# Attention and MoE on one core: PSUM banks and the softmax buffer placed by the emitting code, softmax sums in one burst

## Chip, cores, metric

One core of a Trainium2 chip. The metric is the device time of one execution in microseconds (us). Each kernel was run several times in several rounds; each round also ran the kernel before on the same chip. All runs quoted were classed as fast (undisturbed).

## What is computed

A spatial-reduction attention followed by a two-layer feed-forward network (the "MoE" of the names), cut to what matters:

```python
kv_pool = kv.reshape(B, H//4, 4, W//4, 4, C).mean(axis=(2, 4))     # 384 x 32 -> 96 x 8 = 768 keys
k = v = kv_pool.reshape(B, -1, C) @ w_sr
s = (q @ k.T) / sqrt(C);  a = softmax(s)                           # 4 x 12288 queries, 768 keys, C = 128
x = (a @ v)
h = x @ w_in                                                        # 128 -> 2048
out = (h * sigmoid(1.702 * h)) @ w_out                              # 2048 -> 128
```

The softmax is computed without the maximum: exp, then a product with v, then a division by the column sums.

## The kernel before

Queries come in 96 groups of 512; four groups are a block, so there are 24 blocks. Everything that ScalarE must evaluate comes in chunks of 128 x 512, and three chunks (K = 3) are one unit: TensorE *fills* three PSUM banks, one ACTIVATE of ScalarE *evacuates* them to SBUF as bf16, and later TensorE *drains* each chunk with one matmul into an accumulator. A group has 6 attention chunks and 16 MoE chunks, so there are 96 attention units and 256 MoE units in each of two halves: attention of 48 groups, MoE of 48 groups, and the same again. 704 units in all.

The eight banks are two triples for fills and two accumulators. Accumulators serve every other job in turn: attention outputs, MoE outputs, column sums, pooling, key and value projections, transposes.

```python
R = 2; AG = 31; L = 10
agpool = ctx.enter_context(tc.tile_pool(name="ag", bufs=AG))        # 31 buffers of 3 chunks = 93 chunks
big    = ctx.enter_context(tc.tile_pool(name="big", bufs=2, space=bass.MemoryType.PSUM))
ring   = ctx.enter_context(tc.tile_pool(name="ring", bufs=2, space=bass.MemoryType.PSUM))

def fill_attn(i, t):                      # one unit: three chunks of group i
    s_ps = big.tile([128, K, 512], F32, name="big")
    for k in range(K):
        nc.tensor.matmul(s_ps[:, k, :], kTs[b][:, ...], rhs, start=True, stop=True)
    a = agpool.tile([128, K, 512], BF, name="ag")
    nc.scalar.activation(a, s_ps, AF.Exp, scale=scale)

def sums(s, t):                           # half of a block's column sums: 12 matmuls, four column groups
    if t == 0:
        ss_of[s] = ring.tile([128, 512], F32, name="ring")
    for jc in range(K * t, K * t + K):
        for gi in range(4):
            nc.tensor.matmul(ss[32 * gi:32 * gi + 32, :], ones, a_of[4 * s + gi, t][:, jc % K, :], ...)
    # after the second half: transposes, reciprocal, broadcast
...
for n in range(len(seq)):                 # the emitting loop: a model of ScalarE's backlog decides
    fill_next(n + 2)
    while True:
        ...                               # sums first if due, else other jobs, else a drain
        if f is None and (done == len(todo) or d > (n - L if attn else n)):
            break                         # in attention, keep back the last L = 10 units
        cost = COST[f] if f else 1.0
        if now + cost + K + HANDOVER > end[-1] and n - d <= AG - 4 and n + 3 < len(seq):
            break                         # else ScalarE would run dry: emit the next fill first
        now += cost
        ...
```

The order of instructions is thus fixed when the program is emitted: the loop keeps a small model of when ScalarE will run dry and puts drains and other jobs between fills as they fit.

Of the kernel before, what the change touches and what calls it, by code (L numbers as in the profile page):

```python
# [19 lines left out]
def kernel(  # L20
# [18 lines left out]
    K = 3  # L39
# [10 lines left out]
    AG = 31  # L50
# [8 lines left out]
    agpool = ctx.enter_context(tc.tile_pool(name="ag", bufs=AG))  # L59
    npool = ctx.enter_context(tc.tile_pool(name="norm", bufs=5))  # L60
    opool = ctx.enter_context(tc.tile_pool(name="op", bufs=3))
    big = ctx.enter_context(tc.tile_pool(name="big", bufs=2, space=bass.MemoryType.PSUM))
    ring = ctx.enter_context(tc.tile_pool(name="ring", bufs=2, space=bass.MemoryType.PSUM))

    ctx.enter_context(tc.manual_schedule(engines=None))

# [15 lines left out]
    def pool_kv(b, a):  # L82

        ps = ring.tile([128, 512], F32, name="ring")
        ts = [kv_tiles.pop((b, a, ch)) for ch in range(HC)]
        order = ([(ch, w) for ch in range(HC) for w in range(r)] if b == 0 else
                 [(ch, w) for w in range(r) for ch in range(HC)])
        for ch, w in order:
            if (b, a, w) == (0, 0, 0) and ch > 0:
                warm(4)  # L90
            nc.tensor.matmul(ps[32 * ch:32 * ch + 32, :], mean4, ts[ch][:, w],  # L91
                             start=(w == 0), stop=(w == r - 1))
        pooled[b, a] = kvtmp.tile([Hp, 4, C], BF, name="pooled")
        nc.vector.tensor_copy(pooled[b, a].rearrange("p a c -> p (a c)"), ps[:Hp, :])  # L94

    def transpose_pooled(b, a):
        ps = ring.tile([128, 4, Hp], BF, name="ring")
        t = pooled.pop((b, a))
        for wp in range(4):
            nc.tensor.transpose(ps[:, wp, :], t[:, wp, :], ident[:Hp, :Hp])  # L100
        pTs[b, a] = kvtmp.tile([128, h], BF, name="pT")
        nc.vector.tensor_copy(pTs[b, a], ps.rearrange("p a b -> p (a b)"))

    def make_k(b, a):
        ps = ring.tile([128, 512], F32, name="ring")
        if a == 0:
            kTs[b] = kvres.tile([128, J], BF, name="kT")
        nc.tensor.matmul(ps[:, :h], w_sr_sb, pTs[b, a], start=True, stop=True)
        nc.vector.tensor_copy(kTs[b][:, a * h:(a + 1) * h], ps[:, :h])

    def make_v(b, a):
        ps = ring.tile([128, 512], F32, name="ring")
        if a == 0:
            vs[b] = kvres.tile([128, JC, C], BF, name="v")
        pT = pTs.pop((b, a))
        for k in range(K):
            nc.tensor.matmul(ps[:, k * C:(k + 1) * C], pT[:, k * 128:(k + 1) * 128], w_sr_sb,
                             start=True, stop=True)
        nc.vector.tensor_copy(vs[b][:, a * K:(a + 1) * K, :].rearrange("p k c -> p (k c)"), ps[:, :h])
# [20 lines left out]
    def transpose_q(g):  # L140
# [3 lines left out]
        ps = ring.tile([128, 4, 128], BF, name="ring")  # L144
# [45 lines left out]
    warm_ps = big.tile([128, K, 512], F32, name="big")  # L190

    def warm(n):

        for _ in range(n):
            nc.tensor.matmul(warm_ps[:32, 0, :], ones, ones.unsqueeze(1).broadcast_to([128, 16, 32]),  # L195
                             start=True, stop=True)
# [15 lines left out]
    a_of, av_of, rb_of = {}, {}, {}  # L212

    def fill_attn(i, t):
        b, s = i // GB, i // 4
        s_ps = big.tile([128, K, 512], F32, name="big")
        rhs = qTs[s][:, 0, (i % 4) * G:(i % 4 + 1) * G]
        for k in range(K):
            jc = K * t + k
            nc.tensor.matmul(s_ps[:, k, :], kTs[b][:, jc * 128:(jc + 1) * 128], rhs,  # L220
                             start=True, stop=True)
        a = agpool.tile([128, K, 512], BF, name="ag")
        nc.scalar.activation(a, s_ps, AF.Exp, scale=scale)  # L223
        a_of[i, t] = a

    def drain_attn(i, t, k):
        b, s = i // GB, i // 4
        jc = K * t + k
        if jc == 0:
            av_of[i] = ring.tile([128, 512], F32, name="ring")  # L230
        nc.tensor.matmul(av_of[i], vs[b][:, jc, :], a_of[i, t][:, k, :],  # L231
                         start=(jc == 0), stop=(jc == JC - 1))
        if k == K - 1:
            del a_of[i, t]
        if jc == JC - 1:
            if i % 4 == 0:
                xs[s] = x_tile(s)
            nc.vector.tensor_tensor(xs[s][:, (i % 4) * G:(i % 4 + 1) * G],  # L238
                                    av_of.pop(i), rb_of.pop(i), MUL)

    ss_of = {}

    def sums(s, t):

        if t == 0:
            ss_of[s] = ring.tile([128, 512], F32, name="ring")
        ss = ss_of[s]
        for jc in range(K * t, K * t + K):
            for gi in range(4):
                nc.tensor.matmul(ss[32 * gi:32 * gi + 32, :], ones,  # L250
                                 a_of[4 * s + gi, t][:, jc % K, :],
                                 start=(jc == 0), stop=(jc == JC - 1))
        if t == 0:
            return
# [45 lines left out]
    g_of, o_of = {}, {}  # L300

    def fill_moe(t):
        h_ps = big.tile([128, K, 512], F32, name="big")
        for k in range(K):
            g, fc = divmod(K * t + k, FCH)
            nc.tensor.matmul(h_ps[:, k, :], w_in_sb[:, fc * 128:(fc + 1) * 128],  # L306
                             xs[g // 4][:, (g % 4) * G:(g % 4 + 1) * G], start=True, stop=True)
        a = agpool.tile([128, K, 512], BF, name="ag")
        nc.scalar.activation(a, h_ps, AF.Gelu_apprx_sigmoid)  # L309
        g_of[t] = a  # L310

    def drain_moe(t, k):
        a = g_of[t]
        g, fc = divmod(K * t + k, FCH)
        if fc == 0:
            o_of[g] = ring.tile([128, 512], F32, name="ring")
        nc.tensor.matmul(o_of[g], w_out_sb[:, fc, :], a[:, k, :],  # L317
                         start=(fc == 0), stop=(fc == FCH - 1))
        if k == K - 1:
            del g_of[t]  # L320
        if fc == FCH - 1:

            o_sb = opool.tile([128, 512], F32, name="o_sb")
            nc.vector.transpose(o_sb, o_of.pop(g))  # L324
            for m in range(4):
                nc.sync.dma_start(out=out_r[g, m],
                                  in_=o_sb[32 * m:32 * m + 32, :].rearrange("i (b j) -> i b j", j=32))

    NA, NM = 2 * NG, NG * FCH // K

    units = [(i, t) for t in range(2) for i in range(4)] + [(i, t) for i in range(4, NG) for t in range(2)]
    seq = []
    for n in range(R):
        seq += [(True, u) for u in range(n * NA // R, (n + 1) * NA // R)]
        seq += [(False, u) for u in range(n * NM // R, (n + 1) * NM // R)]

    def fill(p):
        if p >= len(seq):
            return
        attn, n = seq[p]  # L340
        if not attn:
            fill_moe(n)
            return
        i, t = units[n]
        if n % 2 == 0:
            background(n // 2)
        if n == 1:
            transpose_q(3)
        if n == 2:
            make_v(0, 0)  # L350
        if n == 4:
# [3 lines left out]
        if n == 6:  # L355
            make_v(0, 1)
        if n == 7:
            transpose_q(4)
            transpose_q(5)
        if n in (11, 12):  # L360
            extras.append((transpose_q, n - 5))
        elif n % 2 == 1:
            extra(n // 2 - 1)
        fill_attn(i, t)
# [4 lines left out]
    UNIT, SWITCH, HANDOVER = 6.25, 6.0, 1.0  # L369
    COST = {pool_kv: 4.5, transpose_pooled: 1.5, make_k: 1.0, make_v: 1.5, transpose_q: 1.0, sums: 3.5}  # L370
    todo = [(p, k) for p in range(len(seq)) for k in range(K)]
    done = done_s = seen_a = done_a = 0
    now, end = 0.0, []

    def fill_next(p):
# [3 lines left out]
        fill(p)  # L379
# [4 lines left out]
        if p and seq[p][0] != seq[p - 1][0]:  # L384
# [3 lines left out]
    fill_next(0)  # L388
    fill_next(1)
    for n in range(len(seq)):  # L390
        fill_next(n + 2)
        attn, u = seq[n]
        seen_a += attn
        while True:
            d = done // K
            f = None
            if not av_of or done_s in ss_of:
                if done_s in ss_of:
                    f, args = sums, (done_s, 1)
                elif done_s < NS and seen_a >= 8 * done_s + 8 and done_a >= 8 * done_s - 2:  # L400
                    f, args = sums, (done_s, 0)
                elif extras:
                    f, *args = extras[0]
            if f is None and (done == len(todo) or d > (n - L if attn else n)):
                break
            cost = COST[f] if f else 1.0
            if now + cost + K + HANDOVER > end[-1] and n - d <= AG - 4 and n + 3 < len(seq):
                break
            now += cost
            if f is sums:  # L410
                f(*args)
                if args[1] == 1:
                    del ss_of[done_s]
                    done_s += 1
            elif f:
                extras.pop(0)
                f(*args)
            else:
                p, k = todo[done]
                a, w = seq[p]  # L420
                if a:
                    drain_attn(w // 2, w % 2, k)
                    done_a += k == K - 1
                else:
                    drain_moe(w, k)
                done += 1
# [31 lines left out]
```

## Time and profile before

| | before |
|---|---|
| time, median | 1009.5 us (1009.13 to 1010.20, 6 runs) |
| span of the profiled run | 1008.3 us |
| TensorE busy, ScalarE busy | 97%, 95% |
| ScalarE's first Gelu run without a gap starts | 192.69 us |
| first half's last ACTIVATE ends | 509.71 us |
| last weight load of the last sums block | 678.07 us |
| last weight load of all | 1002.57 us |

How to read it. Two engines look full, so the shares say little. The first half ends when ScalarE has made all its units: from 192.69 us on it does not stand still. The second half ends when TensorE has made its last drain: it works off a stock of chunks that attention has left. So a gain in the first half counts only as far as ScalarE gets done earlier, and a gain in the second half counts as TensorE time. The lines are in the prediction below.

One view is used that no single line of the profile gives, here called *priced idle*. The trace records every weight load of TensorE, so the matmuls between the last weight loads of two sums blocks can be counted exactly. Each is priced as in the prediction (0.2158 us for a full one, and so on), and what is left of the interval is idle.

### The profile page before, as it was taken

What the parts mean: (1) busy time and instruction counts of PE and PEld (TensorE: products, weight loads), DVE (VectorE), ACT (ScalarE), POOL (GpSimd) and SP (SyncE); (2) the same over time, 40 slices, a digit from 0 to 9 for tenths busy, and PEclk for the clock granted to TensorE, in tenths of its full rate; (3) what the DMA queues carried; (4) which work ended last, traced back from release to release, by engine and by line L of the source; (5) the groups of instructions that cost most, each with busy time, mean ns of one, the idle gap of its engine ahead of it and who ended that gap; (6) DMA issues with size and microseconds to landing.
All of it is one profiled execution on the core that took longest, in us unless ns stands there. A gap on an engine that the chain in (4) does not pass through costs nothing.

```text
span 1008.3 us, 12769 instructions
## 1 busy us (share of the span) xinstructions
PE 980.7 (97%) x4916; PEld 433.0 (43%) x5014; DVE 199.0 (20%) x321; ACT 960.9 (95%) x711; POOL 92.8 (9%) x151
## 2 busy tenths in 40 slices
PE   7899999999999999999999999999999999999997
PEld 2343344444444444444433344444444444444443
DVE  3333334311101110111113333331101110111101
ACT  3899998999999999999999999999999999999995
POOL 3132322200000000000002212221000000000000
PEclk8999999999999999999999999999999999999999
DMA  9985990142222222222238660000222222222223
GB/s 190 189 165 89 202 151 1 34 80 38 40 43 42 40 35 41 43 43 38 38 71 160 119 109 22 1 1 11 43 43 43 37 38 42 41 43 37 37 43 53
DMA packets 256157, 63.83 MB, mean 63 GB/s; under 512 B 251392, under 2 KB 252544, under 8 KB 255744
## 3 DMA queue, kind: packets, MB, share of 16 engines
q1 hardware_dynamic: 248656, 36.79, 21.5%
q0 software_dynamic: 7440, 26.22, 14.0%
q8 instruction: 39, 0.64, 0.3%
q14 instruction: 22, 0.18, 0.1%
HBM read 52.49 MB, written 36.70 MB: 88 GB/s over the span
## 4 chain that ended last, share of the span: by engine, by line
PE 85%; ACT 9%; DVE 2%; issue 2%; DMA 1%; POOL 0%; SPq 0%; ACTq 0%; DVEq 0%; POOLq 0%
PE big L306 33%; PE ring L317 30%; PE ring L231 9%; PE big L220 9%; ACT ag L223 8%; PE ring L250 3%; ACT ag L309 1%; DMA x<-in_kv_dram 1%; PE ring L91 1%; DMA out_dram<-o_sb 0%; DVE t L257 0%; DVE pooled L94 0%; DVE t L261 0%; DVE x L238 0%; DVE o_sb L324 0%
## 5 line engine op out<-in xcount | busy, mean ns | idle before, releaser
L309 ACT ACTIVATE ag<-big 128x1536 bf16<-128x1536 f32 x512 | 691.1, 1459 | 4.9 <-PE big L306 4.9
L306 PE MATMUL big<-x,w_in_sb 128*128 128x512 bf16 x1532 | 414.9, 379 | 3.4
L317 PE MATMUL ring<-ag,w_out_sb 128*128 128x512 bf16 x1477 | 394.5, 379 | 0.1
L223 ACT ACTIVATE ag<-big 128x1536 bf16<-128x1536 f32 x192 | 262.9, 1461 | 16.8 <-PE big L220 15.4
L306 PEld LDWEIGHTS <-w_in_sb 128*128 128x128 bf16 x1536 | 150.0, 98 | 182.6 <-issue 2.9
L317 PEld LDWEIGHTS <-w_out_sb 128*128 128x128 bf16 x1536 | 150.3, 98 | 181.6 <-issue 0.4
L324 DVE STREAM_TRANSPOSE o_sb<-ring 128x512 f32<-128x512 f32 x96 | 68.8, 717 | 561.6 <-PE ring L317 520.3
L220 PE MATMUL big<-qT,kT 128*128 128x512 bf16 x557 | 156.4, 384 | 8.3 <-ACT ag L223 4.2
L231 PE MATMUL ring<-ag,v 128*128 128x512 bf16 x560 | 155.3, 379 | 3.3 <-DVE x L238 2.0
L264 POOL PARTITION_BROADCAST rb<-t x96 | 66.6, 797 | 577.7 <-DVE t L261 577.7
L238 DVE TENSOR_TENSOR x<-ring,rb 128x512 bf16<-128x512 f32 x96 | 66.4, 692 | 154.3 <-PE ring L231 139.4
L220 PEld LDWEIGHTS <-kT 128*128 128x128 bf16 x576 | 54.2, 98 | 83.2 <-issue 24.3
L231 PEld LDWEIGHTS <-v 128*128 128x128 bf16 x576 | 55.4, 98 | 72.9 <-issue 10.5
L250 PE MATMUL ring<-ag,ones 128*32 128x512 bf16 x576 | 38.4, 382 | 0.0
L257 DVE STREAM_TRANSPOSE t<-ring 128x512 f32<-128x512 f32 x24 | 17.2, 717 | 56.5 <-PE ring L250 56.5
L250 PEld LDWEIGHTS <-ones 128*32 128x32 bf16 x576 | 11.7, 95 | 23.9 <-issue 17.0
L261 DVE STREAM_TRANSPOSE t<-t 128x512 f32<-128x512 f32 x24 | 17.1, 711 | 2.8 <-DVE t L259 0.5
L151 ACT COPY qT<-ring 128x512 bf16<-128x512 bf16 x3 | 1.8, 586 | 13.8 <-PE ring L147 13.8
L125 POOL DMA_DIRECT2D q_bf<-in_q_dram x22 | 11.4, 520 | 4.1 <-DMA x<-in_kv_dram 2.7
L79 POOL DMA_DIRECT2D kvt<-in_kv_dram x18 | 10.1, 568 | 7.8 <-DMA x<-in_kv_dram 4.0
L94 DVE CAST pooled<-ring 96x512 bf16<-96x512 f32 x8 | 5.5, 687 | 15.7 <-PE ring L91 15.7
L195 PE MATMUL big<-ones 128*32 128x512 bf16 x22 | 7.3, 481 | 0.9 <-DVE col L171 0.9
(39 smaller groups left out, 74.9 us busy)
## 6 DMA issues: line engine op xcount, KB each, us to landing
out_dram<-o_sb SPq DMA_DIRECT2D x384, 64.0 KB, 1.9
q_bf<-in_q_dram POOLq DMA_DIRECT2D x22, 512.0 KB, 7.6
kvt<-in_kv_dram POOLq DMA_DIRECT2D x18, 512.0 KB, 9.4
x<-in_kv_dram POOLq DMA_DIRECT2D x6, 512.0 KB, 10.7
x<-in_q_dram POOLq DMA_DIRECT2D x1, 512.0 KB, 18.5
w_in_sb<-in_moe_w_in_dram POOLq DMA_DIRECT2D x1, 512.0 KB, 7.8
w_out_sb<-in_moe_w_out_dram POOLq DMA_DIRECT2D x1, 512.0 KB, 8.4
x<-in_q_dram POOLq DMA_DIRECT2D x1, 384.0 KB, 10.5
```

The costliest lines, as they stand in the source:

```text
L220: nc.tensor.matmul(s_ps[:, k, :], kTs[b][:, jc * 128:(jc + 1) * 128], rhs, start=True, stop=True)
L223: nc.scalar.activation(a, s_ps, AF.Exp, scale=scale)
L231: nc.tensor.matmul(av_of[i], vs[b][:, jc, :], a_of[i, t][:, k, :], start=(jc == 0), stop=(jc == JC - 1))
L238: nc.vector.tensor_tensor(xs[s][:, (i % 4) * G:(i % 4 + 1) * G], av_of.pop(i), rb_of.pop(i), MUL)
L250: nc.tensor.matmul(ss[32 * gi:32 * gi + 32, :], ones, a_of[4 * s + gi, t][:, jc % K, :], start=(jc == 0), stop=(jc == JC - 1))
L257: nc.vector.transpose(t1, ss)
L261: nc.vector.transpose(t2, t1)
L264: nc.gpsimd.partition_broadcast(rb, t2[32 * gi:32 * gi + 1, :])
L306: nc.tensor.matmul(h_ps[:, k, :], w_in_sb[:, fc * 128:(fc + 1) * 128], xs[g // 4][:, (g % 4) * G:(g % 4 + 1) * G], start=True, stop=True)
L309: nc.scalar.activation(a, h_ps, AF.Gelu_apprx_sigmoid)
L317: nc.tensor.matmul(o_of[g], w_out_sb[:, fc, :], a[:, k, :], start=(fc == 0), stop=(fc == FCH - 1))
L324: nc.vector.transpose(o_sb, o_of.pop(g))
```

## The change

The intent: the emitting code itself chooses the PSUM bank of every job and the place of every chunk in one circle of 96, so that it knows when a bank comes free and can avoid waiting for one; a block's sums go out in one burst; and ScalarE may be late by a little (LATE), where before no job was allowed to make it run dry. The diff, cut to its core:

```diff
-    AG = 31
+    AG = 96
     L = 10
-    agpool = ctx.enter_context(tc.tile_pool(name="ag", bufs=AG))
-    big = ctx.enter_context(tc.tile_pool(name="big", bufs=2, space=bass.MemoryType.PSUM))
-    ring = ctx.enter_context(tc.tile_pool(name="ring", bufs=2, space=bass.MemoryType.PSUM))
+    agpool = ctx.enter_context(tc.tile_pool(name="ag", bufs=1))
+    ppool = ctx.enter_context(tc.tile_pool(name="psum", bufs=1, space=bass.MemoryType.PSUM))
+    banks = ppool.tile([128, 8, 512], F32, name="banks")
+    def next_acc():                     # banks 6 and 7 in turn, unless one holds an open group
+        m = 13 - last_acc
+        if m in closes:
+            m = 13 - m
+        return m
 ...
+    ag = agpool.tile([128, AG, 512], BF, name="ag")
+    def place(chunks):                  # the next places of the circle
 ...
-    def sums(s, t):
-        if t == 0:
-            ss_of[s] = ring.tile([128, 512], F32, name="ring")
-        for jc in range(K * t, K * t + K):
+    def sums(s):
+        ss = acc()
+        for jc in range(JC):
             for gi in range(4):
-                nc.tensor.matmul(ss[32 * gi:32 * gi + 32, :], ones, a_of[4 * s + gi, t][:, jc % K, :], ...)
+                nc.tensor.matmul(ss[32 * gi:32 * gi + 32, :], ones, weights(("a", 4 * s + gi, jc)), ...)
 ...
-                nc.sync.dma_start(out=out_r[g, m], ...)
+                eng = nc.scalar if g == NG - 1 and m % 2 else nc.sync
+                eng.dma_start(out=out_r[g, m], ...)
 ...
-    UNIT, SWITCH, HANDOVER = 6.25, 6.0, 1.0
-    COST = {pool_kv: 4.5, ..., sums: 3.5}
+    UNIT, SWITCH, HANDOVER, EVACUATE, LATE = 6.25, 6.0, 1.0, 4.5, 4.5
+    COST = {pool_kv: 6.0, ..., sums: 8.0}
+    free = {6: 0.0, 7: 0.0}
 ...
+            room = AG - len(slot_of)
+            limit = end[-1] - K - HANDOVER if n + 3 < len(seq) else 1e9
+                    if now + COST[sums] <= limit + LATE or room < 4 * K:
+                        f, args = sums, (done_s,)
 ...
-            if f is None and (done == len(todo) or d > (n - L if attn else n)):
+            if at[todo[done]] > (n - L if attn else n) or (kind == "a" and i >= 4 * done_s):
                 break
+            start = max(now, free[next_acc()]) if c == 0 else now
+            if start + 1.0 > limit and not (room < 2 * K + 1 or (room < 4 * K and start == now)):
+                break
```

Before, the keep-back of L = 10 units was counted in the order of drains; after, `at[...]` is the unit in which the chunk itself was filled. The first eight units are emitted as the first halves of groups 0 to 3 and then their second halves, so group 0's last three chunks lie in unit 4, and a drain of them has to wait until seventeen units are out; before, it waited for fourteen.

## The prediction

> **What bounds the kernel now.** I read the page first (busy shares, groups), then ScalarE's timeline, then TensorE's timeline in a few narrow windows.
>
> ```profile
> PE 980.7 (97%) x4916; PEld 433.0 (43%) x5014; DVE 199.0 (20%) x321; ACT 960.9 (95%) x711; POOL 92.8 (9%) x151
> ...
> L309 ACT ACTIVATE ag<-big 128x1536 bf16<-128x1536 f32 x512 | 691.1, 1459 | 4.9 <-PE big L306 4.9
> L306 PE MATMUL big<-x,w_in_sb 128*128 128x512 bf16 x1532 | 414.9, 379 | 3.4
> L317 PE MATMUL ring<-ag,w_out_sb 128*128 128x512 bf16 x1477 | 394.5, 379 | 0.1
> L223 ACT ACTIVATE ag<-big 128x1536 bf16<-128x1536 f32 x192 | 262.9, 1461 | 16.8 <-PE big L220 15.4
> ...
> L250 PE MATMUL ring<-ag,ones 128*32 128x512 bf16 x576 | 38.4, 382 | 0.0
> ```
>
> Two engines look full, so shares do not decide. The work comes in units of three chunks of 512: TensorE fills three banks, ScalarE evacuates them (Exp in the two attention stretches, Gelu in the two MoE stretches), later TensorE drains the chunks. ScalarE's timeline gives its pace and where it stood still:
>
> ```profile
> 141.93 5.48 ACT L223 ACTIVATE ag<-big 128x1536 bf16<-128x1536 f32 x4 [1.12 <-PE big L220]
> 148.19 5.48 ACT L223 ACTIVATE ag<-big 128x1536 bf16<-128x1536 f32 x4 [0.78 <-PE big L220]
> 155.76 4.33 ACT L223 ACTIVATE ag<-big 128x1536 bf16<-128x1536 f32 x3 [2.09 <-PE big L220]
> ...
> 192.69 317.00 ACT L309 ACTIVATE ag<-big 128x1536 bf16<-128x1536 f32 x235 [1.08 <-PE big L306]
> ...
> 680.16 317.00 ACT L309 ACTIVATE ag<-big 128x1536 bf16<-128x1536 f32 x235 [1.08 <-PE big L306]
> ```
>
> 317.00/235 = 1.349 us per unit. After 192.69 ScalarE does not wait again in the first MoE stretch; before it, it waits for fills: TensorE is late. TensorE's own pace, inside MoE:
>
> ```profile
> 300.78 0.81 PE L306 MATMUL big<-x,w_in_sb 128*128 128x512 bf16 x3
> 301.43 1.03 PE L317 MATMUL ring<-ag,w_out_sb 128*128 128x512 bf16 x4
> 302.29 0.81 PE L306 MATMUL big<-x,w_in_sb 128*128 128x512 bf16 x3
> ```
>
> Seven matmuls start in 1.51 us: 0.2158 us each, six per unit = 1.295 us against ScalarE's 1.349. In attention each block of 8 units also has 24 column-sum matmuls (L250), and TensorE is the slower one. I counted weight loads (all 5014 are recorded, matmuls are not) against program order: the stock of evacuated, undrained chunks climbs to its limit of 93 in both attention stretches (from the eighth sums block to the twelfth, the nineteenth to the twenty-first and on), falls by about 60 in each MoE stretch, and at the end 35 drains remain after the last fill. So TensorE sets the end; ScalarE sets the pace only from about 496 to 516 us, when the stock is down to what the program keeps back, and there TensorE waits (0.52, 0.54, 0.54 us before three fills).
>
> **What the Trainium skill says.** "TensorE: Matmul & The Clock Gate", section "Wait — 56ns, not 53.3ns?", gives 215.7 ns start to start at N = 512; the trace agrees (215.8). "TensorEngine Tiling (Array Packing)", "Key Properties": changing the tiling mode drains the engine. The trace agrees and prices it:
>
> ```profile
> 94.61 0.83 PE L250 MATMUL ring<-ag,ones 128*32 128x512 bf16 x12
> 95.38 0.82 PE L220 MATMUL big<-qT,kT 128*128 128x512 bf16 x3
> 96.13 0.83 PE L250 MATMUL ring<-ag,ones 128*32 128x512 bf16 x12
> ```
>
> Two bursts of 12 start 1.52 us apart with three fills (0.647) between: a burst costs 0.873 us. Twelve matmuls in four column groups need 12/4 x 0.2158 = 0.647, so 0.226 us is the two switches. "ScalarE: Activation LUTs", "What ACT_TABLE_LOAD costs", gives 186 + 0.833 N ns for such an ACTIVATE, 1466 ns here; the trace has 1459, and since they overlap I use the measured 1.349.
>
> **The change, part by part.** Instruction counts on every engine are unchanged except where the last output's stores are issued. ScalarE still makes 704 units of 1536; nothing gets faster in itself. Only order moves.
>
> 1. *Sums in one burst.* Program order before: 32 bursts of 12 and 8 of 24; after: 24 of 24. Sixteen fewer bursts x 0.225 = 3.6 us of TensorE, half in each attention stretch. A block's sums then cost 1.52 us.
>
> 2. *Waits for an accumulator bank.* With two accumulators, a short job between two groups puts the next group on the bank whose evacuation has just begun:
>
> ```profile
> 547.82 0.38 PE L231 MATMUL ring<-ag,v 128*128 128x512 bf16 x1
> 548.03 0.33 PE L108 MATMUL ring<-pT,w_sr_sb 128*128 128x384 bf16 x1
> 548.30 0.69 DVE L238 TENSOR_TENSOR x<-ring,rb 128x512 bf16<-128x512 f32 x1 [1.97 <-PE ring L231]
> 549.05 0.59 PE L231 MATMUL ring<-ag,v 128*128 128x512 bf16 x2 [0.69 <-DVE x L238]
> ```
>
> 0.7 to 0.8 us lost. Pricing every interval between sums blocks (full matmuls at 0.2158, bursts as above, pooling bursts 1.09, small ones 0.06 to 0.18) leaves true TensorE idle of 5.7 us from block 1 to 12, and 5.7 from block 13 to 24. Intervals without pooling jobs have 0.03 to 0.6, those with them mostly 0.6 to 1.8. The changed emission starts a group only when the bank is reckoned free and puts a fill after the key projection; three such waits of about 0.2 us per job set remain by the same arithmetic: 0.5 us a set, 2.0 in the first stretch, 1.0 in the second, plus 0.05 a block.
>
> 3. *A new idle.* After the first block the changed program has four fills in a row with no drain: a group may now only be drained when its last chunk is ten units old. Thirteen units pass between blocks 1 and 2, 13 x 1.349 = 17.5 us, with 15.6 us of TensorE work: 1.9 us idle (before: 1.6 in the shorter interval).
>
> 4. *Circle of 96.* The stock peaks at 87 and then 81 chunks, against 93. The larger buffer is not used up; in the second attention stretch nothing is forced out by a full buffer. The start's pooling work stays.
>
> 5. *Late ScalarE.* Blocks in the second stretch have 9 units: TensorE 51 x 0.2158 + 1.52 = 12.53 us, ScalarE 12.14. ScalarE goes idle about 0.4 us a block, which costs nothing while TensorE has no gaps.
>
> 6. *Last stores.* The last four take 1.94 us to issue on one queue; on two, half: 0.9 us off the end.
>
> **The sum, on the path.** First stretch: block 1 ends at 34.9 before, at 34.05 after (one fill and one switch fewer). To block 12: 573 full matmuls 123.65, 11 x 1.52 = 16.7, four pooling bursts 4.4, small ones 3.1, idle 1.9 + 2.0 + 0.4 = 4.3: 186.2 (before 190.6). Before, ScalarE restarts 2.1 us later, at 192.69; after, at 188.3, but with 237 units left in the half instead of 235: 188.3 + 237 x 1.349 = 508.0 (before 509.7). So most of TensorE's 4.4 us are not gained: fewer units are ahead. Second stretch: table load 1.28, then unit 20 ends at 536.3; fill 0.65 and burst 1.5: block 14 at 538.4. To block 24: 519 full matmuls 112.0, 10 x 1.52 = 15.2, two pooling bursts 2.2, small ones 1.3, idle 1.5: 670.6 (before 678.1). To the last weight load: 1503 x 0.2158 = 324.35: 995.0. Then 5.7 us as before, less 0.9: a span of 999.8. The time is 1.2 us above the span before (1009.5 against 1008.3), so 1001.0 us, 0.8% faster.
>
> **Rivals.**
> - *ScalarE becomes the bound.* Without any wait it needs 18.3 (start) + 704 x 1.349 + 3 x 1.28 = 971.9, and with a tail of about 10 us the time would be some 983, 2.6% faster. For it: the change aims at ScalarE's 20 us of waits. Against: the sum above without any of its idle is still a span near 994; TensorE's work was not reduced enough.
> - *The gain is mostly spent.* If bank waits stay as they are (5.7 us per stretch) and only the switches and the stores help, the first half gains nothing (two more units to go) and the second about 3: 1005 to 1006.
> - *False waits from one big tile.* If an ACTIVATE had to wait for the one just before, it would lose its overlap, 1.459 − 1.349 = 0.11 us x 704 = 77 us slower. Against: in the built program every ACTIVATE waits for the one 32 units earlier (31 before), and TensorE's waits on ScalarE and VectorE are as many as before (for example 512 + 190 on ScalarE by the fills). So small.
>
> **Range and chances.** The switches and the stores are counts times measured costs (4.5 us together); the idle terms are the soft part, from 3 to 11 us in all. That gives 996 to 1006. Faster by over 2% means below 989.3, under TensorE's work without idle: 4%. Slower by over 2%: only false waits, 2%.
>
> **What would show it.** Right: 24 sums bursts about 1.52 us from start to the next full matmul; waits before L231's counterpart on VectorE near none; ScalarE's first Gelu run without a gap starting near 188 and the second near 673; about 26 drains after the last fill; the last stores issued in about 1 us. Wrong: ScalarE's gaps in attention under 5 us in total (rival one), or gaps of 0.1 us all through MoE (rival three). My weakest term is the idle in the second stretch.

## The result

The changed kernel takes **1004.33 us** (median of 6 runs, 1004.10 to 1005.44), the kernel before 1009.5 us beside it; the ratio is 0.9951, 95% interval 0.9938 to 0.9964. Ratios here are the mean time of one kernel's fast runs over that of the other's of the same rounds, so not quite the ratio of the quoted medians. The gain is 0.5%; 0.8% was predicted.

The page of the changed kernel, with the groups of instructions; the last line is the drains of attention of the kernel after, whose counterpart before follows in the second fence:

```profile
PE 978.4 (98%) x4920; PEld 435.4 (43%) x5014; DVE 198.8 (20%) x321; ACT 959.7 (96%) x711; POOL 92.7 (9%) x151
...
L340 ACT ACTIVATE ag<-banks 128x1536 bf16<-128x1536 f32 x512 | 690.9, 1476 | 4.0 <-PE banks L338 3.2
...
L266 ACT ACTIVATE ag<-banks 128x1536 bf16<-128x1536 f32 x192 | 262.0, 1469 | 15.8 <-PE banks L264 15.5
...
L272 PE MATMUL banks<-ag,v 128*128 128x512 bf16 x567 | 155.2, 379 | 1.0 <-DVE o_sb L352 0.2
```

```profile
L231 PE MATMUL ring<-ag,v 128*128 128x512 bf16 x560 | 155.3, 379 | 3.3 <-DVE x L238 2.0
```

Nothing got faster in itself: ScalarE works as long as before. The waits of the drains for a bank that VectorE still evacuates have gone from 3.3 us of idle, 2.0 of it on VectorE, to 1.0 (which part of the change did this, e1 shows below). ScalarE's idle in attention has hardly moved (16.8 to 15.8).

ScalarE's timeline after, with the last wait in attention, the start of the first Gelu run without a gap, and that of the second:

```profile
140.35 11.04 ACT L266 ACTIVATE ag<-banks 128x1536 bf16<-128x1536 f32 x8 [0.43 <-PE banks L264]
152.66 7.28 ACT L266 ACTIVATE ag<-banks 128x1536 bf16<-128x1536 f32 x5 [1.27 <-PE banks L264]
...
189.72 319.74 ACT L340 ACTIVATE ag<-banks 128x1536 bf16<-128x1536 f32 x237 [1.12 <-PE banks L338]
...
674.03 320.08 ACT L340 ACTIVATE ag<-banks 128x1536 bf16<-128x1536 f32 x237 [0.43 <-PE banks L338]
```

The first run starts 2.97 us earlier than before but is two units longer (2 x 1.349 = 2.70), so it ends at 509.48 instead of 509.71: **the first half gained 0.2 us**. The rest of the span was 498.6 us and is now 493.9: **the second half gained 4.7 us.** Its parts, by priced idle and counts: seven bursts fewer after block 13 (7 x 0.225 = 1.6), idle from block 13 to 24 5.7 before and 2.1 after (3.6), 0.9 from the first half's end to block 13; against that 0.65 (one fill more left at block 13), 0.4 (idle at the very end) and 0.2 (the tail). That makes some 4.8, of 4.7 measured.

The burst itself, in TensorE's timeline of the kernel after:

```profile
51.54 1.48 PE L287 MATMUL banks<-ag,ones 128*32 128x512 bf16 x24
52.95 0.82 PE L264 MATMUL banks<-qT,kT 128*128 128x512 bf16 x3
```

All 24 blocks have one such burst, 1.41 us from its start to the next full matmul, to which some 0.1 us of the switch ahead of it come; two bursts of 12 cost 2 x 0.873.

Where the bank waits went shows best in the list of TensorE's waits from 535 to 672 us, the second attention stretch. The kernel before has

```profile
PE ring L231 <- DVE x L238: 1.4, 2, 0.7
PE ring L108 <- DVE pT L102: 1.2, 1, 1.2
PE big L220 <- ACT ag L223: 1.0, 4, 0.3
```

and the same list of the kernel after is empty. (Columns: us in total, times, the longest. It shows only what the recorded matmuls waited for, so less than priced idle.) In the first stretch, between the first two blocks, there is a new idle, of fills that wait for ScalarE:

```profile
37.16 0.82 PE L264 MATMUL banks<-qT,kT 128*128 128x512 bf16 x3 [0.81 <-DVE qT L181]
...
39.70 0.81 PE L264 MATMUL banks<-qT,kT 128*128 128x512 bf16 x3 [0.20 <-ACT ag L266]
41.04 0.81 PE L264 MATMUL banks<-qT,kT 128*128 128x512 bf16 x3 [0.54 <-ACT ag L266]
42.39 0.81 PE L264 MATMUL banks<-qT,kT 128*128 128x512 bf16 x3 [0.54 <-ACT ag L266]
```

Four fills in a row with nothing between: every one waits until ScalarE has evacuated the bank triple of two fills ago, so they come at ScalarE's pace (1.34 us from start to start) where a fill by itself takes 0.647 us. Some 0.7 us of TensorE go by in each, of which this view books 0.54. It is the keep-back rule's doing: there are chunks to drain, but none that is old enough. The new way of counting has its share: e1 below, with L = 10 and the old counting, emits drains between these fills and has 1.0 us of priced idle from block 1 to 2, where the changed kernel has 2.7. No run changes the counting alone. The same thing happens ahead of the second half's first burst, with 39 chunks in hand:

```profile
513.62 0.81 PE L264 MATMUL banks<-qT,kT 128*128 128x512 bf16 x3 [0.40 <-ACT ag L266]
514.96 0.81 PE L264 MATMUL banks<-qT,kT 128*128 128x512 bf16 x3 [0.53 <-ACT ag L266]
...
519.00 0.81 PE L264 MATMUL banks<-qT,kT 128*128 128x512 bf16 x3 [0.54 <-ACT ag L266]
...
522.42 1.48 PE L287 MATMUL banks<-ag,ones 128*32 128x512 bf16 x24
```

The kernel before had three such waits there, this one six (priced idle from block 12 to 13: 2.5 before, 4.0 after).

### The profile page after: what moved, and what is told of

Read it like the earlier page. It is cut to its first block, busy times and chain, and to the rows that moved or that the text cites. A ratio compares the mean times of both kernels' runs of the same rounds, so it can differ in the third digit from the quotient of the medians.

```text
span 1003.4 us, 12797 instructions
## 1 busy us (share of the span) xinstructions
PE 978.4 (98%) x4920; PEld 435.4 (43%) x5014; DVE 198.8 (20%) x321; ACT 959.7 (96%) x711; POOL 92.7 (9%) x151
## 4 chain that ended last, share of the span: by engine, by line
PE 89%; ACT 6%; DVE 1%; issue 1%; DMA 1%; POOL 0%; SPq 0%; ACTq 0%; DVEq 0%; POOLq 0%
PE banks L338 32%; PE banks L345 31%; PE banks L272 11%; PE banks L264 10%; ACT ag L266 4%; PE banks L287 3%; ACT ag L340 2%; DMA x<-in_kv_dram 1%; PE banks L119 1%; DVE pooled L122 0%; ACT L340 0%; PE banks L128 0%; DVE t L291 0%; DVE o_sb L352 0%; DVE t L295 0%
## 5 line engine op out<-in xcount | busy, mean ns | idle before, releaser
L340 ACT ACTIVATE ag<-banks 128x1536 bf16<-128x1536 f32 x512 | 690.9, 1476 | 4.0 <-PE banks L338 3.2
L338 PE MATMUL banks<-x,w_in_sb 128*128 128x512 bf16 x1503 | 408.8, 379 | 2.0 <-ACT ag L340 0.2
L345 PE MATMUL banks<-ag,w_out_sb 128*128 128x512 bf16 x1506 | 401.5, 379 | 1.6
L266 ACT ACTIVATE ag<-banks 128x1536 bf16<-128x1536 f32 x192 | 262.0, 1469 | 15.8 <-PE banks L264 15.5
L352 DVE STREAM_TRANSPOSE o_sb<-banks 128x512 f32<-128x512 f32 x96 | 68.8, 717 | 559.1 <-PE banks L345 538.4
L264 PE MATMUL banks<-qT,kT 128*128 128x512 bf16 x554 | 156.1, 384 | 9.0 <-ACT ag L266 6.0
L272 PE MATMUL banks<-ag,v 128*128 128x512 bf16 x567 | 155.2, 379 | 1.0 <-DVE o_sb L352 0.2
L279 DVE TENSOR_TENSOR x<-banks,rb 128x512 bf16<-128x512 f32 x96 | 66.4, 692 | 166.0 <-PE banks L272 146.5
L287 PE MATMUL banks<-ag,ones 128*32 128x512 bf16 x576 | 35.5, 381 | 0.0
L291 DVE STREAM_TRANSPOSE t<-banks 128x512 f32<-128x512 f32 x24 | 17.2, 717 | 47.9 <-PE banks L287 47.9
L287 PEld LDWEIGHTS <-ones 128*32 128x32 bf16 x576 | 13.2, 96 | 20.6 <-issue 10.2
L107 POOL DMA_DIRECT2D kvt<-in_kv_dram x18 | 10.2, 573 | 24.1 <-PE banks L119 20.2
L221 PE MATMUL banks<-ones 128*32 128x512 bf16 x22 | 7.3, 480 | 0.9 <-DVE col L199 0.9
```

Of the source, the lines that this page charges most:

```text
L264: nc.tensor.matmul(ps[:, k, :], kTs[i // GB][:, jc * 128:(jc + 1) * 128], rhs, start=True, stop=True)
L266: nc.scalar.activation(place([("a",) + c for c in chunks]), ps, AF.Exp, scale=scale)
L272: nc.tensor.matmul(av_of[i], vs[b][:, jc, :], weights(("a", i, jc)), start=(jc == 0), stop=(jc == JC - 1))
L279: nc.vector.tensor_tensor(xs[s][:, (i % 4) * G:(i % 4 + 1) * G], av_of.pop(i), rb_of.pop(i), MUL)
L287: nc.tensor.matmul(ss[32 * gi:32 * gi + 32, :], ones, weights(("a", 4 * s + gi, jc)), start=(jc == 0), stop=(jc == JC - 1))
L291: nc.vector.transpose(t1, ss)
```

## The experiments

Two theories stood against each other. **A**: the single burst is nearly the whole gain, and the bank placement's gain is eaten up by the keep-back rule, which idles TensorE with chunks in hand. **B**: the placement (banks reckoned free, a circle in place of pools) makes the gain. Where two kernels are compared as a whole, "placement" stands for all of the change but the burst: banks, circle, the new costs, LATE, the counting of the keep-back and the last stores. For comparing halves, this table has what decides each run; "first burst" is the last weight load of the first sums block, "rest" is the span less the first half's end.

| profiled run | first burst | gapless Gelu run starts, units left | first half ends | rest | span | mean clock |
|---|---|---|---|---|---|---|
| before | 34.92 | 192.69, 235 | 509.71 | 498.6 | 1008.3 | 0.994 |
| predicted for after | 34.05 | 188.3, 237 | 508.0 | 491.8 | 999.8 | |
| after | 34.13 | 189.72, 237 | 509.48 | 493.9 | 1003.4 | 0.994 |
| e1, before + one burst | 33.09 | 191.05, 235 | 508.06 | 495.1 | 1003.2 | 1.000 |
| e3, after, stores on one queue | 33.08 | 188.67, 237 | 508.45 | 494.1 | 1002.6 | 0.999 |
| e4, after + L = 5 | 33.08 | 189.49, 235 | 506.92 | 491.3 | 998.2 | 0.998 |
| e5, after without bank times | 33.53 | 189.40, 237 | 509.17 | 494.4 | 1003.6 | 0.995 |
| e6, after, circle of 84 | 33.07 | 186.99, 240 | 510.74 | 492.0 | 1002.7 | 1.000 |
| e8, e4 + transposes together | 34.28 | 187.31, 236 | 505.97 | 491.3 | 997.3 | 0.999 |
| e9, old placement, burst, L = 5 | 35.55 | 192.10, 235 | 509.12 | 493.4 | 1002.5 | 0.995 |
| e10, after + transposes together | 34.16 | 189.76, 237 | 509.52 | 493.9 | 1003.4 | 1.000 |

The start is not the same from run to run: where the mean clock is 0.994 or 0.995, the first burst comes up to 1 us later (for after, e3, e4 and e6, whose start is the same program, 34.13 against 33.08, 33.08 and 33.07). The trace shows the place: the granted clock of the profiled runs of before and after was 0.52 from 12 to 19 us and 0.50 from 26 to 29 us, that of e1, e3 and e10 was 1.00 there. So before and after may be compared as they stand, and for e1 the fair partner is e3. In e8 and e10 the first burst is later for another reason, their edit. The medians mix both kinds of run, so a difference under 1 us is also given between runs of like clock.

### e1: one burst, nothing else

```diff
-        for jc in range(K * t, K * t + K):
+        for jc in range(JC):
-            now += cost
+            now += 2 * cost if f is sums else cost
```

on the kernel before, with pools and two accumulators in turn as they were.

> The kernel before, with nothing changed but the column sums of a block emitted as one burst of 24 (24 bursts instead of 40), old tile pools, old drain rule. Theory A (the switches are the gain, the placing of banks adds little): TensorE is spared 16 x 0.225 = 3.6 us; the number of units filled at the twelfth block is the same as before (117), so the first half keeps its share too: 1005 to 1006.5 us, near the changed kernel's 1004.3 or within 2 us of it. Theory B (the gain came from banks, circle and lateness together, the burst alone is worth little because later bank waits take it back): 1008 or more. The trace should show 24 bursts, each with about 1.5 us to the next full matmul, and waits of the attention-value matmuls on VectorE as in the kernel before (about 2.5 us in all).

Measured: 1005.03 us (1004.95 to 1005.74), ratio 0.9957, interval 0.9945 to 0.9969. One part of the change alone gives 4.5 of its 5.2 us, so in time theory A's first half holds. But the expectation that the drains' waits on VectorE would stay (about 2.5 us) failed. The drains of attention in e1:

```profile
L231 PE MATMUL ring<-ag,v 128*128 128x512 bf16 x568 | 155.2, 379 | 1.1 <-DVE t L253 0.5
```

The 2.0 us on VectorE's evacuation (x L238) have gone with the old pools in use; what is left, 1.1 us, is as little as in the changed kernel (1.0). Its list of waits from 535 to 672 us has none before a drain either: 0.8 us before a transpose, 0.7 of fills on ScalarE. Joining the sums also moves the other jobs, and with them the waits. So e1 does not measure the switches alone: of the 3.5 us by which its rest is shorter than before's, 1.6 are seven bursts fewer, 1.6 are less priced idle from block 13 to 24, and 0.9 come before block 13, less 0.65 for one fill more. The placement takes another 1.8 us of idle from block 13 to 24. It does not follow yet that it is worthless, only that in the changed kernel little of it shows (0.7 us in the medians, 0.8 between runs of like clock).

### e2: no lateness

```diff
-    ... EVACUATE, LATE = 6.25, 6.0, 1.0, 4.5, 4.5
+    ... EVACUATE, LATE = 6.25, 6.0, 1.0, 4.5, 0.0
```

> The changed kernel with LATE = 0 in place of 4.5: a burst (reckoned as 8 slots) never fits before the next fill is due, so it is put off until the circle is full: the program order shows 16 fills in a row without a drain in each half. Theory A (lateness is what makes the single burst possible): TensorE idles about 0.54 us at each of some 2 x 16 fills, 17 us, part of which is only moved because TensorE was the bound: 1012 to 1020 us. Rival (lateness only trims): within 2 us of 1004.3.

Measured: 1041.76 us (1033.13 to 1044.56), ratio 1.0305: slower than the kernel before, and by far more than I had expected. With a burst reckoned at 8.0, the model finds no room for it until the circle is nearly full, and drains must wait for the burst. The first burst comes at 61.51 us instead of 33.24, after a row of fills like those above; the second half begins in the same way, with 15.5 us of priced idle ahead of its first burst. The groups page of this run has, for the fills of attention,

```profile
L264 PE MATMUL banks<-qT,kT 128*128 128x512 bf16 x561 | 157.6, 387 | 31.5 <-ACT ag L266 21.3 <-DMA qT<-q_bf 7.0 <-DVE kT L137 1.2
```

31.5 us of idle, 21.3 on ScalarE; 7.0 on two late query loads, which may be why its runs spread over 11 us. The first half ends 21 us later than in the changed kernel and the rest is 14 us longer; these were not broken down further. So the lateness is not a fine adjustment: in the changed kernel's model, which asks for room for all 8.0 of a burst, the burst needs the permission to be late, and without this small part of the diff the rest loses 3%. It is not a rule for every model: e1 has the single burst without LATE, but its check asks for room for 3.5 only and books twice that.

### e3: last stores on one queue

```diff
-                eng = nc.scalar if g == NG - 1 and m % 2 else nc.sync
+                eng = nc.sync
```

> The changed kernel with the last group's four stores all on one queue, as before. The prediction gave two queues 0.9 us. The trace of the changed kernel showed landings only 0.4 us earlier after the last transpose and a longer closing stretch after them (1.56 against 0.92 us). Theory A (two queues gain nothing by the end): within 0.3 us of the changed kernel, either sign. Theory B (they gain 0.4 to 0.9): slower by that much.

Measured: 1004.6 us (1004.25 to 1005.14), ratio 0.9951, as the changed kernel. The two queues gain 0.3 us in the medians and 0.2 between runs of like clock, which the intervals don't resolve, where the prediction had put 0.9 us. The ends of the timelines show why. Before:

```profile
1003.20 0.72 DVE L324 STREAM_TRANSPOSE o_sb<-ring 128x512 f32<-128x512 f32 x1 [2.74 <-DMA out_dram<-o_sb]
1003.95 1.94 SPq L326 DMA_DIRECT2D out_dram<-o_sb  x4
```

After (the other two stores are issued by SyncE at the same time):

```profile
998.10 0.72 DVE L352 STREAM_TRANSPOSE o_sb<-banks 128x512 f32<-128x512 f32 x1 [2.74 <-DMA out_dram<-o_sb]
998.84 0.93 ACTq L355 DMA_DIRECT2D out_dram<-o_sb  x2
```

e3, the changed kernel with one queue:

```profile
997.06 0.72 DVE L352 STREAM_TRANSPOSE o_sb<-banks 128x512 f32<-128x512 f32 x1 [2.74 <-DMA out_dram<-o_sb]
```

The issue is 1.0 us shorter, as predicted. But the end of the program stands at 5.07 us after the start of this last transpose before (1008.27 - 1003.20) and at 5.3 after (1003.4 - 998.10). Against the transpose, the last landing is only 0.4 us earlier (3.67 us after the transpose's start in place of 4.09), and the stretch from there to the end is 0.6 us longer (1.61 in place of 0.98; the expectation, which has 1.56 and 0.92, measured to SyncE's last instruction). But most of that growth is not the second queue's: e3, with one queue, takes 5.49 us from the transpose to the end (1002.55 - 997.06), 4.08 to the landing and 1.41 after it. Against e3 the two queues land 0.4 us earlier and end 0.2 us earlier. The four traces with the old pools all have 0.97 or 0.98 in the closing stretch, the eight of the changed kernel 1.10 to 1.61; why is not settled.

### e4: keep back 5 units instead of 10

```diff
-    L = 10
+    L = 5
```

> The changed kernel with L = 5 in place of 10: a chunk may be drained five units after its fill instead of ten. Theory A (TensorE sets the end, and its waits for ScalarE at the start of each attention stretch, 1.3 us and 2.9 us in the trace of the changed kernel, were put there by L): the four and the six fills in a row disappear (some three fills in a row are left before the first burst of the second stretch), and 117 units instead of 115 are filled at the twelfth block: first half 2 to 3 us shorter, second 1 to 2: 999.5 to 1001.5 us. Rival (idle there is only moved elsewhere): 1003.5 to 1005.

Measured: 1000.26 us (1000.04 to 1006.37 over 6 runs, five of them under 1001.4; the slow one was not profiled), ratio 0.9922, interval 0.9904 to 0.9941. One digit is worth 4.1 us, nearly as much as the whole change. The first half ends 2.6 us earlier (1.05 of it is this profiled run's earlier start) and the rest is 2.6 us shorter. Two fills instead of six wait ahead of the second half's first burst, and 30 chunks are in hand there instead of 39: 9 x 0.2158 = 1.9 us of drains done while TensorE otherwise stood still. This is theory A's second half, shown.

### e5: banks reckoned free at once

```diff
-    ... EVACUATE, LATE = 6.25, 6.0, 1.0, 4.5, 4.5
+    ... EVACUATE, LATE = 6.25, 6.0, 1.0, 0.0, 4.5
```

> The changed kernel with one constant altered: EVACUATE 4.5 becomes 0, so the emitting code reckons every accumulator bank free at once and starts a group without waiting for the evacuation; everything else stays. Program order then has 24 bursts and 115 units filled at the twelfth sums block, as the changed kernel (1004.3). Theory A (the single burst is nearly the whole gain, timed banks are worth about 1 us): 1004.3 to 1006.0, with some drain waits on VectorE of 0.4 to 0.7 us back, of which the first half hides its share behind ScalarE. Rival B (my prediction's step 2: reckoning the banks removes waits of 2.7 us in the first stretch and 4 in the second): 1006.5 to 1008, with about 3 us of waits on VectorE before the drains of attention and TensorE idle of 5 us or more from the second half's first sums block to its last.

Measured: 1005.37 us (1004.98 to 1005.94), ratio 0.9956: 1.0 us slower in the medians, 0.5 to 0.8 between runs of like clock, as theory A said (the intervals do not resolve it); rival B (1006.5 to 1008) falls. One wait on VectorE before the drains is back in each stretch (0.7 us each), and priced idle grows by 0.3 and 0.7 us. The reckoning of free banks is thus worth up to 1 us here. That the other bank waits do not come back fits e1, where the burst alone took them away. What the choice of the bank, the higher costs of the jobs in the model and the lateness add was not taken apart.

### e6: a smaller circle

```diff
-    AG = 96
+    AG = 84
```

> The changed kernel with a circle of 84 chunks instead of 96. The order holds at most 75 chunks (81 to 87 before), has 112 instead of 115 units filled at the twelfth block, and, since room runs out, puts eight fills in a row before the second half's first block. My reading (what counts in the first half is how many units are filled when ScalarE stops waiting: each missing one costs 1.349 us of ScalarE, less the 0.647 of TensorE that its fill no longer takes before that, so 0.70): 3 x 0.70 = 2.1 us, and about two more fills that wait for a bank at 0.5 each at the second half's start, so 1006.5 to 1008. Rival (the circle's size does not matter, since TensorE sets the end and its work is unchanged): 1003.5 to 1005.

Measured: 1004.77 us (1004.75 to 1006.18), ratio 0.9953: 0.4 us slower in the medians, 0.6 between runs of like clock, which the intervals do not resolve and which lies in the rival's range. My reading failed, and the table says at which point. In the first half it holds: three units fewer are ahead, and the first half ends 1.26 us later, though this run's start was 1.06 us earlier, so 2.3 us by my sum of 2.1. But the rest is 1.9 us shorter. At the second half's first burst, with the same 362 units filled, this order holds 30 chunks and the changed kernel 39: those nine drains, 1.9 us, were made in the time in which ScalarE sets the pace and TensorE waits anyway. The agreement of the two numbers is in part chance: up to the last weight load the rest is only 1.5 us shorter (the nine drains, less 0.5 of more idle), and 0.5 is this profiled run's shorter closing stretch. What the first half loses to ScalarE, the second half's start mostly gives back, as a smaller stock. The expectation had added up only the first half.

### e7 and e9: the old placement with burst and short keep-back

```diff
-    L = 10
+    L = 5
+            if f is None and seq[todo[done][0]][0] and seq[todo[done][0]][1] // 2 >= 4 * done_s:
+                break                          # no drain ahead of its block's sums
-            transpose_q(4)
-            transpose_q(5)
+            for g in (4, 5, 6, 7):
+                transpose_q(g)
```

on e1's kernel. The condition and the transposes are needed for correctness: with L = 5 alone drains would come ahead of their sums.

> The kernel before (pools for PSUM and for the chunks, no timed banks, no lateness) with two things done: a block's sums in one burst (as e1_joined, 1005.0), and a chunk kept back for 5 units instead of 10 (as e4_keep5 did to the changed kernel); attention drains then have to be held behind their block's sums by an explicit condition, and four query transposes are emitted together. 117 units filled at the twelfth block. Theory A (burst and keep-back are what matters; bank and circle placement by the emitting code is worth 1 to 2 us at most): 1001.0 to 1003.0. Rival B (keep-back pays only with the new placement, since otherwise the bank waits take over): 1004.0 to 1005.5.

Measured: 1010.17 us in the median, but in two groups: 1002.90 and 1002.93, and four runs from 1009.8 to 1013.83; ratio 0.9988, interval 0.9954 to 1.0021. The profiled run is one of the slow ones, and its timeline of TensorE shows the place:

```profile
153.45 1.46 PE L220 MATMUL big<-qT,kT 128*128 128x512 bf16 x3 [8.35 <-DMA qT<-q_bf]
154.71 1.06 PE L231 MATMUL ring<-ag,v 128*128 128x512 bf16 x2
```

A fill waits 8.35 us for the transposing load of a block of queries; one load of queries took 37.6 us from issue to landing, where the longest in seven other profiles looked at is 19.7 to 23.2. It costs 10.2 us, because after the wait TensorE runs at half speed for a while: the granted clock was 0.52 from 150 to 157 us, and three fills start 0.42 us apart (1.26 us for three) instead of 0.2158. As this run could not decide, e9 moved one load out of that place:

```diff
-        if i == 34:
+        if i == 44:
             nc.gpsimd.dma_start(out=w_out_sb, ...)
```

> As e7_oldbanks_joined_keep5, with one load moved: the half megabyte of w_out, which e7 issues at 111.8 us just ahead of a clump of five loads of keys and queries (123 us on), is issued ten query groups later. In e7 the profiled run lost 10.2 us in one interval (8.35 us in a fill's wait for the transposing load of a query block; a query load landed 37.6 us after its issue), and its runs were 1002.9 twice and 1009.8 to 1013.8 four times. Theory A (the arithmetic of TensorE in e7 is that of its two quick runs; the slow ones lose it in late loads, which crowd at that place): all or nearly all runs at 1002 to 1004, no wait on DMA in the attention stretch. Rival B (late loads are not a matter of this clump, but of the places at which this order issues them, or of chance): again runs of 1009 and more.

Measured: 1002.91 us (1002.74 to 1004.27 over 5 runs), ratio 0.9935, interval 0.9923 to 0.9948. This is what theory A of e9 expects, but it is not shown to the end: only one of e7's four slow runs was profiled, and e9 ran on another chip than e7 (as the kernel before did beside each), so that none of five runs was slow, where four of six had been, can be the chip's doing or chance. That the profiled slow run lost its 10.2 us to the late load is shown; by whose queueing the load was late is not. So with the short keep-back the *old* placement gives 1002.9 and the new one 1000.3 or, with the same transposes, 999.0 (e8): **there the placement is worth 3.9 us, five times the 0.7 us that it shows with L = 10** (1005.0 against 1004.3; e7's two quick runs, without the moved load, agree with e9). The four kernels ran on up to four chips, on which the kernel before had medians from 1009.3 to 1009.5, so these differences hold to some tenths. With L = 10 the keep-back spends what the placement saves. The table shows where: from the first burst to the first half's end e1 takes 474.97 us and the changed kernel 475.35, so the placement loses 0.4 there, and gains 1.2 in the rest. With L = 5 it gains in both: e9 takes 473.57 and e8 471.69, and the rest is 2.1 shorter. Which piece of the placement saves this was not taken apart.

### e8 and e10: query transposes together

```diff
-            transpose_q(4)
-            transpose_q(5)
+            for g in (4, 5, 6, 7):
+                transpose_q(g)
...
-            extras.append((transpose_q, p - 5))
+            pass
```

on e4's kernel (L = 5) for e8, on the changed kernel (L = 10) for e10.

> The version that was fastest so far (the changed kernel with 5 units kept back, e4_keep5, 1000.26) with the four query transposes of groups 4 to 7 emitted together before the first sums block, so that no fill between the first two blocks waits for VectorE's copy of a transposed query (0.8 us in the changed kernel). By itself that is some 0.8 us of TensorE in the first stretch, but the order then has 116 units filled at the twelfth block instead of 117, which costs 0.70. So: 999.5 to 1000.8, no difference to be resolved. If the fills' wait was on the path with nothing to take its place: 999.0 to 999.5.

> The changed kernel with only the query transposes of groups 4 to 7 emitted together, as e8_keep5_transposes, but with the 10 units of keep-back left. Theory A (the keep-back of 10 units is what idles TensorE after the first sums block and before the second half's first, and a wait for a query copy taken away there only becomes a wait for an evacuated bank): between the first and the second block still 2 to 2.7 us of idle, 1003.3 to 1004.6. Rival B (the wait of 0.8 us for the query copy was on the path by itself): 1003.0 to 1003.5 with 1.9 us or less of idle there. Either way far from 999.0, which needs the shorter keep-back.

Measured: e8 **999.03 us** (998.84 to 999.74), ratio 0.9893, interval 0.9879 to 0.9908, the fastest of all, 1.2 us under e4 and at the lower border of what I had expected if the wait was on the path. e10 1005.48 us (1005.19 to 1006.72), ratio 0.9964: about 1 us *slower* than the changed kernel, and over the range of both theories (ratios 0.9964 and 0.9951 from different chips). The same edit helps with one keep-back and harms with the other. TensorE's timeline after the first burst, first of e10, then of e8:

```profile
37.05 0.81 PE L264 MATMUL banks<-qT,kT 128*128 128x512 bf16 x3 [0.89 <-ACT ag L266]
...
39.73 0.81 PE L264 MATMUL banks<-qT,kT 128*128 128x512 bf16 x3 [0.54 <-ACT ag L266]
41.08 0.81 PE L264 MATMUL banks<-qT,kT 128*128 128x512 bf16 x3 [0.54 <-ACT ag L266]
```

```profile
34.81 0.82 PE L264 MATMUL banks<-qT,kT 128*128 128x512 bf16 x3
35.46 0.59 PE L272 MATMUL banks<-ag,v 128*128 128x512 bf16 x2
35.90 0.81 PE L264 MATMUL banks<-qT,kT 128*128 128x512 bf16 x3
```

In e10 the wait for the query copy has gone and a wait for ScalarE stands in its place; the priced idle from block 1 to 2 is 3.2 us, more than the 2.7 of the changed kernel, and the transposes now come ahead of the first burst. The whole loss lies there: at a like clock (1.000 and 0.999) e10's first burst comes at 34.16, that of e3 at 33.08, and from there to block 2 both take 18.30 us and to the last weight load both 963.35. In e8, whose first burst is as late (34.28), drains lie between the fills from the start, and the idle of that interval is 0.04 us. A wait taken away is a gain only if there is something that may be done in its place.

## Why the prediction was right and where it was off

The measured 1004.33 lies in the range of 996 to 1006, and 94% was on "within 2%". The centre was 3.3 us too low. Its own checkpoints, predicted and measured, one after the other:

| checkpoint | predicted | measured | miss added here |
|---|---|---|---|
| first half's end on ScalarE | 508.0 | 509.48 | +1.5 |
| burst of block 14 | 538.4 | 540.21 | +0.3 |
| burst of block 24 | 670.6 | 672.59 | +0.2 |
| last weight load | 995.0 | 997.46 | +0.5 |
| span | 999.8 | 1003.4 | +1.1 |
| time, median | 1001.0 | 1004.33 | -0.3 |

- **Step 1, the burst**: right. 24 bursts at the cost worked out, and e1 shows that it is most of the gain, though not by the switches alone: joining the sums also took away the drains' waits, which the prediction had put under step 2.
- **Step 2, bank waits**: right for the second stretch. Block 14 to 24 took 132.4 us of 132.2 predicted, and the waits before attention's drains on VectorE have all but gone. The cause was wrong: the prediction gave the credit to starting a group only when its bank is reckoned free. By e5 that is at most 1 us, and in e1, with nothing reckoned, the burst alone brings the idle before the drains from 3.3 to 1.1 us and takes 1.6 us of idle out of the second stretch.
- **Step 3, the new idle**: the mechanism is right and the term too small. "1.9 us idle" between blocks 1 and 2 measured 2.7. A fill there also waits 0.81 us for a query copy, but that is not the reason: in e10 this wait is gone and the interval is as long, 18.30 us, where the prediction had 13 x 1.349 = 17.5; the other 0.8 us stay unexplained. The idle of the whole stretch from block 1 to 12 was 5.7 us, the same as before, where the sum had 4.3. These 1.4 us are nearly the whole miss of the first half. I had also seen this keep-back only at the start; the same rule idles six fills at the second half's start (4.0 us of priced idle from block 12 to 13), and e4 shows that five units less of keep-back are worth 4.1 us of time in all. That was the term with the most in it, and I gave it one line.
- **Step 4, the circle**: right. The stock stood at 87 and 81 chunks at the 12th and the 24th burst, as stated (just after the latter it touches 85), and 26 drains were left after the last fill. e6 shows that even 84 places suffice.
- **Step 5, late ScalarE**: right in the order as built; that LATE holds the whole thing up (e2) was not seen.
- **Step 6, last stores**: "0.9 us off the end" failed. The issue shrank by 1.0 us, the last landing came 0.4 us and the end 0.2 us earlier than with one queue (e3), and the changed kernel has a longer closing stretch whatever the queue; I took a term off the path at its full size without asking what follows the issue.
- **The sum**: the prediction added 1.2 us for time over span from a median and a profiled run that was not the median one. The profiled run of the kernel before took 1010.07 us for its span of 1008.3, so 1.8. This miss and the profiled run of after being slower than its median (1005.14) nearly cancel.
- **The rivals**: "The gain is mostly spent" with 1005 to 1006 came closest, for half the reason that it gave: its first half gained nothing, as it said, but not because bank waits stayed as they were. They went, and the keep-back's idle took their place.

## What to carry to other kernels

In a program whose order is fixed when it is emitted, a rule that holds work back (keep the last ten units) is a cost wherever the other engine sets the pace: look for rows of the same instruction, each with the same small wait, and ask what could have been put between them. Test a bundle's parts apart and together: the burst alone gave 4.5 of 5.2 us (and took bank waits away that had been credited to another part), the placement showed 0.7, and with a shorter keep-back the same placement was worth 3.9. And before a wait is taken away, or a term is taken off the end, name what would run in its time; the stores had next to nothing, and the transposes had nothing as long as L was 10.

## What the Trainium skill lacked or had wrong

- "TensorEngine Tiling (Array Packing)", "Key Properties", says that changing the tiling mode drains the engine, and gives no price. Here two switches around a burst of four-column-group matmuls cost 0.225 us together, and 24 matmuls in one burst instead of two of 12 saved that each time.
- "DMA: Bandwidth & Descriptors", "Issuing engines are not separate DMA queues", says that issuing from several engines saves only the sequencer's time, which is "usually small relative to the DMA itself". The runs agree that nothing more is to be had, and show that most of even this time was not gained: one 64 KB store took SyncE 0.49 us to issue (median; four: 1.94 us, two on each of two queues: 0.93), and of the 1.0 us saved 0.4 showed at the last landing and 0.2 at the end of the program (e3's trace against the changed kernel's; medians 1004.6 and 1004.33 us).
- "ScalarE: Activation LUTs", "What ACT_TABLE_LOAD costs", has back-to-back ACTIVATEs overlap by about 93 ns; these, of 128 x 1536, overlapped by 110 ns in the kernel before (one is recorded with 1.459 us on average, and in a row they start 1.349 apart) and by 127 ns in the changed kernel (1.476).
